# Attention scores of a head pair as two 64-row matmuls, each head with a PSUM bank of its own

## The chip, the cores and the metric

The kernel runs on one core of a Trainium2 chip. The metric is the device time of one execution in microseconds (us). Engines are named as the profile names them: PE (TensorE matmuls), PEld (TensorE weight loads), DVE (VectorE), ACT (ScalarE), POOL (GpSimd), SP (SyncE, which issues the DMAs).

## The reference

Three blocks follow each other. First comes an attention over 2 batches, 8 heads, 768 positions and a head dimension of 64: each query sees the keys within 15 positions of its own, and 24 summary keys (the maximum over blocks of 32 keys) with log(32) added to their scores.

```python
k_sum = k.reshape(B, H, nb, block, D).max(axis=3)
v_sum = v.reshape(B, H, nb, block, D).mean(axis=3)
scores_l = scale * np.matmul(q, k.transpose(0, 1, 3, 2))
scores_s = scale * np.einsum('bhsd,bhnd->bhsn', q, k_sum) + np.log(block)
scores_all = np.concatenate([np.where(mask_l, scores_l, -1e9), scores_s], axis=-1)
a = softmax(scores_all)
out = np.matmul(a, np.concatenate([v, v_sum], axis=2))
```

Then 1536 tokens of width 512 go through an RMS norm, a gated layer (silu(x w_gate) * (x w_val)) w_out with 1536 hidden units, and a second layer (s * relu(x w_in)^2 + b) w_out with 2048 hidden units. All is float32, the weights are float64 in memory.

## The kernel before

**Work units.** A token tile i is 128 queries of one batch (12 tiles). A unit is a token tile and a pair of heads (4 pairs, so 48 units). The queries and keys of a pair lie with the first head in partitions 0 to 63 and the second in 64 to 127. A unit's key window has 192 columns: 24 summary keys, 8 empty ones, two times 16 neighbours and the tile's own 128 keys.

**Scores (`emit_a`, line 317).** The queries lie in `qz` (line 79), two buffers of [128, 2, 4, 128]: for head e of the pair, the other head's 64 rows are zero, set once in `consts` (lines 113 to 115). `load_q` (line 268) fills a tile's queries with two DMAs of 64 rows. Per unit, line 328 issues two float32 matmuls over all 128 rows, one per head, into the two halves of one PSUM bank. A float32 matmul that isn't a transpose stands in the trace as two weight loads and two matmul records, so a unit has four of each. Then `top` (line 333, on DVE) adds the mask, scales and takes the row maximum of each head, and `exps` (line 339, on ACT) does the exponentials and their sums.

**Order of the work.** `attn` (line 405) runs over steps s. A step first issues, three steps late, the transposes of unit s-3 (`emit_b`, line 348, copied out by line 354 on ACT or 352 on DVE), then, six steps late, the products with the values (`emit_c`, lines 367 to 369), and yields; then it issues the scores of unit s and yields again. At each yield the main loop (line 640) calls `run_due`, which issues the work that `after(d, ...)` put d calls later: `top` at the second call after the scores, `exps` at the third. It then may issue a transpose of a normed tile (`emit_e`, line 396) and one group of 12 matmuls of the gated layer (lines 469 to 472). Each engine works through its own instructions in the order of issue.

**PSUM banks.** The scores take banks 0, 1 and 2 in turn, and from the 20th yield on banks 0 and 1 in turn (lines 631 and 644). A unit's matmuls wait until the `top` of the unit that last used their bank has read it. The transposes use 3, 4 and 5 (later 3 and 4), the value products 6 and 7, the layers 2 and 5.

**Other work of the engines.** On DVE: block maxima of the keys (line 276) and sums of the values (line 292), the norm (379, 389), half of the split of normed tokens (402), and the conversion of float64 weights (192 to 194). On ACT: lines 183, 214, 354, 383, 400, 509. On POOL: 216, 313, 358, 359, 385. After the attention's last unit only the two layers run, up to the end.

```python
ps = ps_s()
pv = [ps[:, e * KC:(e + 1) * KC] for e in range(2)]
for e in range(2):
    nc.tensor.matmul(pv[e], qz[i % 2][:, e, pr], kW(i // NTL, pr, t), start=True, stop=True)
```

Of the kernel before, what the change touches and what calls it, by code (L numbers as in the profile page):

```python
# [9 lines left out]
F32 = mybir.dt.float32  # L10
# [3 lines left out]
AF = mybir.ActivationFunctionType  # L14
ALU = mybir.AluOpType
AX = mybir.AxisListType
PSUM = bass.MemoryType.PSUM
# [3 lines left out]
NPAIR = NH // 2  # L21
NTL = SEQ // 128
# [3 lines left out]
KC = 192  # L26
# [10 lines left out]
def kernel(ctx: ExitStack, tc: tile.TileContext, q_t, k_t, v_t, v_w, w_gate, w_val, w_out, w_in2, w_out2, rms_g, s2, b2, out):  # L37
    nc = tc.nc
    scale = 1.0 / math.sqrt(HD)
# [16 lines left out]
    psp = pool("ps", 1, space=PSUM)  # L56

    def banks(*ids):
        """tiles of the PSUM banks ids, in turn"""
        turn = [0]  # L60

        def take():
            i = ids[turn[0] % len(ids)]
            turn[0] += 1
            return psp.tile([128, 512], F32, tag=f"b{i}", name=f"b{i}")
        return take
# [1 line left out]
    def r(ap):  # L68
        return ap.bitcast(F32R)

# [1 line left out]
    ident = const.tile([128, 128], F32, name="ident")  # L72
    mone = const.tile([128, NH], F32, name="mone")
    mhalf = const.tile([128, 1], F32, name="mhalf")
# [1 line left out]
    gbc = const.tile([128, DM], F32, name="gbc")  # L76
    sbc = const.tile([128, 1], F32, name="sbc")
    bbc = const.tile([128, 1], F32, name="bbc")
    qz = [const.tile([128, 2, NPAIR, 128], F32, name=f"qz{i}") for i in range(2)]
    part = const.tile([128, NSUB * 4 * SUB], F32, name="part")  # L80

    def big():
        return hgp.tile([128, NSUB * 2 * SUB], F32, tag="hg", name="hg")

    # keys and values of both batches lie where the products of the MoE come to lie later
    store = [big() for _ in range(5)] + [part[:, i * 3072:(i + 1) * 3072] for i in range(2)]
    kst = [t.rearrange("p (j c) -> p j c", c=KC) for t in (store[0], store[3], store[5])]
    vst = [t.rearrange("p (t a c) -> p t a c", t=3, a=NPAIR) for t in (store[1], store[2], store[4], store[6])]
# [2 lines left out]
    def kW(b, pr, t):  # L91
        j = (b * NPAIR + pr) * NTL + t
        return kst[j // 16][:, j % 16]

    def kpieces(b, pr):
        """runs of tiles of a pair's keys in one store: (store, slot, first tile, tiles)"""
        j = (b * NPAIR + pr) * NTL
        out, t = [], 0
        while t < NTL:
            n = min(NTL - t, 16 - (j + t) % 16)  # L100
            out.append((kst[(j + t) // 16], (j + t) % 16, t, n))
            t += n
        return out
# [6 lines left out]

    def consts():
        make_identity(nc, ident)
        for z in qz:
            nc.vector.memset(z[64:128, 0], 0.0)
            nc.vector.memset(z[0:64, 1], 0.0)
        for st in kst:
            nc.vector.memset(st[:, :, NS:BLK], 0.0)
        m = masks[1]
        nc.gpsimd.memset(m, 0.0)
        nc.gpsimd.memset(m[:, 0:NS], math.log(BLK) / scale)  # L120
        nc.gpsimd.memset(m[:, NS:BLK], NEG / scale)
        band(m, BLK, WIN, -WIN)
        band(m, BLK + WIN, WIN, 128)
        band(m, 64, 128, 0)
        for i, o in ((0, BLK), (2, BLK + WIN)):
            nc.vector.tensor_copy(masks[i], m)
            nc.vector.memset(masks[i][:, o:o + WIN], NEG / scale)
        nc.gpsimd.memset(mhalf, -0.5)
        nc.gpsimd.memset(mone, -1.0)
# [3 lines left out]
        nc.sync.dma_start(out=sbc, in_=s2.rearrange("(o d) -> o d", o=1).broadcast_to([128, 1]))  # L133
        nc.sync.dma_start(out=bbc, in_=b2.rearrange("(o d) -> o d", o=1).broadcast_to([128, 1]))

# [1 line left out]
    later = [[] for _ in range(8)]  # L137

    def after(d, fn):
        later[d].append(fn)  # L140
# [4 lines left out]
        for fn in due:  # L145
            fn()

# [1 line left out]
    order = []  # L149
    for m in range(KF):  # L150
        order.append(("s1", m))
# [26 lines left out]
        raw_t[i] = t  # L178

    def w_scale(i):  # L180
        """high words as float32 with their exponent moved: 2^-112 leaves five bits of it"""
        a = wap.tile([128, 512], F32, tag="wa", name="wa")
        nc.scalar.activation(out=a, in_=raw_t[i][:, :, 1].bitcast(F32), func=AF.Copy, scale=2.0 ** -112)
        a_t[i] = a

    def w_bits(i):
        """float32 of the float64 words: 23 bits of mantissa, the last one rounded to odd"""
        t = raw_t.pop(i)
        lo, hi = t[:, :, 0], t[:, :, 1]
        ai = a_t[i].bitcast(I32)  # L190
        ops = [
            lambda: nc.vector.tensor_scalar(out=ai, in0=ai, scalar1=3, scalar2=1, op0=ALU.logical_shift_left, op1=ALU.bitwise_or),
            lambda: nc.vector.scalar_tensor_tensor(out=ai, in0=hi, scalar=-0x80000000, in1=ai, op0=ALU.bitwise_and, op1=ALU.bitwise_or),  # L193
            lambda: nc.vector.scalar_tensor_tensor(out=ai, in0=lo, scalar=29, in1=ai, op0=ALU.logical_shift_right, op1=ALU.bitwise_or),  # L194
        ]
        pend[i] = ops

        def one():
            if ops:
                ops.pop(0)()  # L200
        one()
        if busy[0]:
            after(1, one)
            after(3, one)
        else:
            one()
            one()
# [27 lines left out]
                prog[j] += 1  # L235

    def w_ahead(part):
        """the weights' own work, between the work of the tokens"""
        i = used[0]
        if part == 0:  # L240
            w_to(i + 8, i + 7, 0, i + 5)
        elif part == 1:
            w_to(i + 8, 0, i + 6, 0)
# [6 lines left out]
        used[0] += 1  # L250
        return ready.pop(i)

# [1 line left out]
    vt_t = {}  # L254

    def load_k(b, pr):
# [9 lines left out]
        nc.sync.dma_start(out=vA[b][t].rearrange("p a c -> p (a c)"), in_=v_w[b, t])  # L266

    def load_q(i):
        z = qz[i % 2]
        for e in range(2):  # L270
            nc.sync.dma_start(out=z[64 * e:64 * e + 64, e].rearrange("p a c -> p (a c)"), in_=q_t[i, 64 * e:64 * e + 64])

    def prep_k(b, pr):
        ks = smallp.tile([128, NS], F32, tag="ks", name="ks")
# [10 lines left out]
        return vt_t[b][:, c0:c0 + 512].rearrange("p (a c) -> p a c", a=NPAIR)  # L285

    def prep_v(b, pr):
        """block means of the values, per column of the transposed values"""
        if pr == 0:
            nc.gpsimd.memset(vsums(b, 0), 0.0)  # L290
        vs = vsums(b, 1)[:, :, 0:NS]
        nc.vector.tensor_reduce(out=vs[:, pr], in_=vt_t[b][:, pr * SEQ:(pr + 1) * SEQ].rearrange("p (c i) -> p c i", i=BLK),
                                axis=AX.X, op=ALU.add)
        if pr == NPAIR - 1:
            for h in range(2):
                p0 = 64 * h
                nc.scalar.activation(out=vsums(b, 0)[p0:p0 + 64, :, p0:p0 + NS], in_=vs[p0:p0 + 64], func=AF.Copy, scale=1.0 / BLK)
# [16 lines left out]

    P_t, PT_t, X_t, xn_t, sm_t = {}, {}, {}, {}, {}

    def emit_a(i, pr, ps_s):
        t = i % NTL
        mk = masks[0 if t == 0 else 2 if t == NTL - 1 else 1]
        if pr == 0:  # L320
            sm_t[i] = smallp.tile([128, 2, NH], F32, tag="sm", name="sm")
        sm = sm_t[i]
        P = (tmpp.tile([128, 512], F32, tag="tmp", name="P") if i else wlp.tile([128, 512], F32, tag="wl", name="P"))
        P = P[:, 0:2 * KC].rearrange("p (e c) -> p e c", e=2)
        ps = ps_s()
        pv = [ps[:, e * KC:(e + 1) * KC] for e in range(2)]
        for e in range(2):
            nc.tensor.matmul(pv[e], qz[i % 2][:, e, pr], kW(i // NTL, pr, t), start=True, stop=True)  # L328

        def top():  # L330
            for e in range(2):
                h = 2 * pr + e
                nc.vector.tensor_tensor_reduce(out=P[:, e], in0=pv[e], in1=mk, op0=ALU.add, op1=ALU.min,
                                               scale=-scale, scalar=3.0e38, accum_out=sm[:, 0, h:h + 1])

        def exps():
            for e in range(2):
                h = 2 * pr + e
                nc.scalar.activation(out=P[:, e], in_=P[:, e], func=AF.Exp, scale=-1.0,  # L339
                                     bias=sm[:, 0, h:h + 1], accum_out=sm[:, 1, h:h + 1])  # L340
        after(1, top)
        after(2, exps)
        P_t[i, pr] = P

    def emit_b(i, pr, ps):
        P = P_t.pop((i, pr)).rearrange("p e c -> p (e c)")
# [55 lines left out]
        after(1, lambda: nc.vector.tensor_tensor(out=r(x[:, 1, :, c0:c0 + 128]), in0=pv, in1=x[:, 0, :, c0:c0 + 128], op=ALU.subtract))  # L402

    def attn(ps_s, ps_t, ps_x):
        """half a unit per step; yields the token tile that it completes"""
        loads = [lambda t=t: load_vw(0, t) for t in range(3, NTL)]
        loads += [lambda pr=pr: load_k(1, pr) for pr in range(NPAIR)]
        loads.append(lambda: load_vt(1))
# [31 lines left out]
        for s in range(n + LC):  # L440
# [14 lines left out]
                        emit_d(i)  # L455
            yield done
            if s < n:
                emit_a(*us[s], ps_s)
                i, pr = us[s]
                if pr == NPAIR - 1 and i + 2 < NT:  # L460
                    load_q(i + 2)
                yield

# [1 line left out]
    def mm12(ps, w, act):  # L465
        hi, lo = w
        for kk in range(4):
# [4 lines left out]
            nc.tensor.matmul(ps, r(hi[:, kk * 128:(kk + 1) * 128]), r(act(kk, 1)), start=False, stop=kk == 3)  # L472

    def slot(part):
        """what follows a group of products: the weights ahead, then older groups' work"""
        run_due()
        if phase:
            part = phase[0] = 1 - phase[0]
        if not busy[0]:
            w_ahead(part)  # L480
# [6 lines left out]
        return big().rearrange("p (s e c) -> p s e c", s=NSUB, e=2)  # L487

    def two(ps, dst, bias=None):
        """ps (+ bias) as a float32r pair"""  # L490
        if bias is None:
            nc.scalar.activation(out=r(dst[0]), in_=ps, func=AF.Copy)
            nc.vector.tensor_tensor(out=r(dst[1]), in0=ps, in1=dst[0], op=ALU.subtract)
# [2 lines left out]
            nc.vector.scalar_tensor_tensor(out=r(dst[1]), in0=ps, scalar=bias, in1=dst[0], op0=ALU.add, op1=ALU.subtract)  # L496

    def moe(x, ps_m):
        """x: a tile of (hi, lo) per part of the tokens"""
        hs, gs, y = {}, {}, []  # L500
        yp = part.rearrange("p (m s c) -> p m s c", m=KD, s=NSUB)
        op = part.rearrange("p (t c) -> p t c", t=NT)
# [112 lines left out]
        for kind, m in order:  # L615
            yield from {"s1": s1, "s2": s2, "s3": s3, "s4": s4}[kind](m)

# [1 line left out]
    consts()  # L619
    x = [xyp.tile([128, 2, KD, SUB], F32, tag="xy", name="x")]  # L620
    load_k(0, 0)
# [6 lines left out]
    for t in range(3):  # L628
        load_vw(0, t)
    load_small()  # L630
    m_banks, s_banks, t_banks = [banks(2, 5)], [banks(0, 1, 2)], [banks(3, 4, 5)]

    def ps_t():
        return t_banks[0]()
# [49 lines left out]
def _layout(q, k, v, moe_w_gate, moe_w_val, moe_w_out, moe_rms_g, moe2_w_in, moe2_w_out, moe2_s, moe2_b):  # L684
# [2 lines left out]
    c = np.ascontiguousarray  # L687

    def heads(a):
        # [b, h, s, d] -> [b, (e d), pair, s]  # L690
        return a.reshape(NB, NPAIR, 2, SEQ, HD).transpose(0, 2, 4, 1, 3).reshape(NB, 128, NPAIR, SEQ)

    qt = heads(q).reshape(NB, 128, NPAIR, NTL, 128).transpose(0, 3, 1, 2, 4)
# [63 lines left out]
```

## Time and profile before

| what | value |
|---|---|
| time, median of 2 runs (lowest to highest) | 663.58 us (663.47 to 663.69) |
| profiled execution: span from first to last instruction | 662.4 us |
| what the times have around that span (663.58 - 662.4) | 1.2 us |
| PE busy in the span | 645.8 us (97%) |
| DVE, ACT, POOL busy | 402.2, 272.6, 137.3 us |
| mean granted TensorE clock | 0.997 |
| score matmuls (line 328), first and last start | 7.8 and 113.9 us |

The profiled execution has a span and no time of its own beside it; the 1.2 us is what the measured runs have more than this span. Busy times of one engine can overlap with another's. A matmul's record is longer than its pitch, because matmuls are pipelined: the pitch is read from the starts.

### The profile page before, as it was taken

How to read it: one execution, taken by the hardware profiler on the slowest of the kernel's cores; microseconds unless marked ns; L12 is line 12 of the kernel's file. 1: busy time of each engine (PE TensorE's matmuls, PEld its weight loads, DVE VectorE, ACT ScalarE, POOL GpSimd, SP SyncE). 2: the span in 40 equal slices, each digit the busy share in tenths (PEclk: the TensorE clock that was granted, in tenths of full speed). 3: DMA queues.
4: the chain of work that ended last, by engine and by line, in shares of the span. 5: the costliest groups of instructions: out<-in, count | busy, mean ns of one | idle time of the engine just before them, and what ended most of it. 6: DMA issues, size and time to landing. Idle time of an engine off the chain costs nothing.

```text
span 662.4 us, 8488 instructions
## 1 busy us (share of the span) xinstructions
PE 645.8 (97%) x3140; PEld 547.7 (83%) x3140; DVE 402.2 (61%) x763; ACT 272.6 (41%) x610; POOL 137.3 (21%) x157
## 2 busy tenths in 40 slices
PE   3989999999999999999999999999999999999998
PEld 3988999888888888888888888888888888888886
DVE  7699777469751355554455767882178637854632
ACT  3888767235433333321233335552455035403400
POOL 2365633213211111111111111110221022102100
PEclk9999999999999999999999999999999999999999
DMA  9995230014332121222222212113022202220022
GB/s 299 301 347 167 65 120 9 0 45 147 95 96 63 33 64 64 64 63 66 63 69 62 71 53 64 65 63 96 0 96 64 95 13 84 65 63 1 1 95 96
DMA packets 23243, 56.13 MB, mean 85 GB/s; under 512 B 2465, under 2 KB 8865, under 8 KB 23201
## 3 DMA queue, kind: packets, MB, share of 16 engines
q1 hardware_dynamic: 23200, 55.58, 26.4%
q8 instruction: 25, 0.41, 0.3%
q14 instruction: 18, 0.14, 0.1%
HBM read 52.43 MB, written 3.15 MB: 84 GB/s over the span
## 4 chain that ended last, share of the span: by engine, by line
PE 91%; ACT 2%; DMA 2%; DVE 2%; POOL 1%; issue 1%; SPq 0%; POOLq 0%
PE b L469 21%; PE b L470 21%; PE b L472 21%; PE b L601 7%; PE b L604 7%; PE b L602 7%; PE b L328 3%; DMA qz<-in_q_t_dram 2%; PE b L348 1%; ACT P L339 1%; PE b L367 1%; PE b L369 1%; PE b L368 1%; PE b L396 1%; ACT PT L354 0%
## 5 line engine op out<-in xcount | busy, mean ns | idle before, releaser
L216 POOL TENSOR_TENSOR wl<-wa,wh 128x512 fp32r<-128x512 f32 x68 | 90.5, 1338 | 418.4 <-ACT wh L214 328.8
L469 PE MATMUL b<-x,wh 128*128 128x512 f32 x288 | 113.1, 393 | 0.0
L470 PE MATMUL b<-x,wl 128*128 128x512 f32 x288 | 112.1, 389 | 0.0
L214 ACT ACTIVATE wh<-wa 128x512 fp32r<-128x512 f32 x68 | 41.5, 626 | 90.8 <-PE b L604 45.5
L472 PE MATMUL b<-x,wh 128*128 128x512 f32 x288 | 77.1, 389 | 0.0
L602 PE MATMUL b<-wl,hg 128*128 128x512 f32 (+1 forms) x196 | 75.1, 385 | 0.0
L601 PE MATMUL b<-wh,hg 128*128 128x512 f32 (+1 forms) x196 | 75.1, 385 | 0.0
L469 PE MATMUL b<-y,wh 128*128 128x512 f32 x192 | 74.7, 389 | 0.0
L470 PE MATMUL b<-y,wl 128*128 128x512 f32 x192 | 74.7, 389 | 0.0
L583 DVE SCALAR_TENSOR_TENSOR b<-u,sbc 128x512 f32<-128x512 f32 x48 | 50.7, 1056 | 35.6 <-ACT u L582 35.6
L472 PEld LDWEIGHTS b<-x,wh 128*128 128x128 f32 x288 | 54.1, 188 | 11.3
L470 PEld LDWEIGHTS b<-x,wl 128*128 128x128 f32 x288 | 54.1, 188 | 11.0
L469 PEld LDWEIGHTS b<-x,wh 128*128 128x128 f32 x288 | 54.1, 188 | 11.0
L469 PE MATMUL b<-hg,wh 128*128 128x512 f32 x144 | 56.0, 389 | 0.0
L470 PE MATMUL b<-hg,wl 128*128 128x512 f32 x144 | 56.0, 389 | 0.0
L496 DVE SCALAR_TENSOR_TENSOR hg<-b,bbc,hg 128x512 fp32r<-128x512 f32 x48 | 35.9, 749 | 28.2 <-ACT hg L495 28.2
L604 PE MATMUL b<-wh,hg 128*128 128x512 f32 (+1 forms) x196 | 51.5, 385 | 0.0
L472 PE MATMUL b<-y,wh 128*128 128x512 f32 x192 | 51.3, 389 | 0.0
L610 DVE TENSOR_TENSOR part<-b,part 128x512 f32<-128x512 f32 (+1 forms) x37 | 24.4, 673 | 43.4 <-PE b L604 43.4
L495 ACT ACTIVATE hg<-b,bbc 128x512 fp32r<-128x512 f32 x48 | 33.0, 688 | 43.0 <-DVE b L583 43.0
L194 DVE SCALAR_TENSOR_TENSOR wa<-raw,wa 128x512 int32<-128x512 int32 x68 | 49.2, 724 | 2.1
L193 DVE SCALAR_TENSOR_TENSOR wa<-raw,wa 128x512 int32<-128x512 int32 x68 | 49.1, 722 | 2.3
(93 smaller groups left out, 1075.0 us busy)
## 6 DMA issues: line engine op xcount, KB each, us to landing
raw<-in_w_out_dram SPq DMA_DIRECT2D x28, 512.0 KB, 3.5
raw<-in_w_in_dram SPq DMA_DIRECT2D x16, 512.0 KB, 3.5
raw<-in_w_gate_dram SPq DMA_DIRECT2D x12, 512.0 KB, 3.8
raw<-in_w_val_dram SPq DMA_DIRECT2D x12, 512.0 KB, 3.5
hg<-in_v_w_dram SPq DMA_DIRECT2D x9, 512.0 KB, 7.7
qz<-in_q_t_dram SPq DMA_DIRECT2D x24, 128.0 KB, 4.8
vt<-in_v_t_dram SPq DMA_DIRECT2D x8, 384.0 KB, 6.5
out_dram<-part SPq DMA_DIRECT2D x11, 256.0 KB, 2.0
```

The source lines that it names most:

```text
L193: lambda: nc.vector.scalar_tensor_tensor(out=ai, in0=hi, scalar=-0x80000000, in1=ai, op0=ALU.bitwise_and, op1=ALU.bitwise_or),
L194: lambda: nc.vector.scalar_tensor_tensor(out=ai, in0=lo, scalar=29, in1=ai, op0=ALU.logical_shift_right, op1=ALU.bitwise_or),
L214: nc.scalar.activation(out=r(h), in_=a, func=AF.Copy)
L216: nc.gpsimd.tensor_tensor(out=r(lo), in0=a, in1=h, op=ALU.subtract)
L469: nc.tensor.matmul(ps, r(hi[:, kk * 128:(kk + 1) * 128]), xh, start=kk == 0, stop=False)
L470: nc.tensor.matmul(ps, r(lo[:, kk * 128:(kk + 1) * 128]), xh, start=False, stop=False)
L472: nc.tensor.matmul(ps, r(hi[:, kk * 128:(kk + 1) * 128]), r(act(kk, 1)), start=False, stop=kk == 3)
L496: nc.vector.scalar_tensor_tensor(out=r(dst[1]), in0=ps, scalar=bias, in1=dst[0], op0=ALU.add, op1=ALU.subtract)
L583: after(0, lambda u=u, ps=ps: nc.vector.scalar_tensor_tensor(out=ps, in0=u, scalar=sbc[:, 0:1], in1=u, op0=ALU.mult, op1=ALU.mult))
L601: nc.tensor.matmul(acc, gh, r(ws[e][0][:, cs]), start=e == 0, stop=False)
L602: nc.tensor.matmul(acc, gh, r(ws[e][1][:, cs]), start=False, stop=False)
L604: nc.tensor.matmul(acc, r(ge[e][:, 1]), r(ws[e][0][:, cs]), start=False, stop=e == 3)
```

## The change

Both heads' queries lie in one buffer without zeros, loaded by one DMA per tile. At every even unit, `emit_a` takes both score banks and issues the scores of two units (pairs pr0 and pr0+1): for each pair, head 0 from partitions 0 to 63 into bank `pe[0]`, and head 1 from partitions 64 to 127 into bank `pe[1]`. The second unit's maxima are issued one `run_due` after the first's, its exponentials likewise, so that they come one call earlier than before, where its scores were issued one step later. The scores rotate over banks 0 and 1 from the start. Docstrings and comments also go; they are left out here.

```diff
-    qz = [const.tile([128, 2, NPAIR, 128], F32, name=f"qz{i}") for i in range(2)]
+    qz = [const.tile([128, NPAIR, 128], F32, name=f"qz{i}") for i in range(2)]
...
-        for z in qz:
-            nc.vector.memset(z[64:128, 0], 0.0)
-            nc.vector.memset(z[0:64, 1], 0.0)
...
     def load_q(i):
-        z = qz[i % 2]
-        for e in range(2):
-            nc.sync.dma_start(out=z[64 * e:64 * e + 64, e].rearrange("p a c -> p (a c)"), in_=q_t[i, 64 * e:64 * e + 64])
+        nc.sync.dma_start(out=qz[i % 2].rearrange("p a c -> p (a c)"), in_=q_t[i])
...
-    def emit_a(i, pr, ps_s):
+    def emit_a(i, pr0, ps_s):
...
-        ps = ps_s()
-        pv = [ps[:, e * KC:(e + 1) * KC] for e in range(2)]
-        for e in range(2):
-            nc.tensor.matmul(pv[e], qz[i % 2][:, e, pr], kW(i // NTL, pr, t), start=True, stop=True)
+        pe = [ps_s() for _ in range(2)]
+        for j in range(2):
             for e in range(2):
+                rows = slice(64 * e, 64 * e + 64)
+                nc.tensor.matmul(pe[e][:, j * KC:(j + 1) * KC], qz[i % 2][rows, pr0 + j], kW(i // NTL, pr0 + j, t)[rows],
+                                 start=True, stop=True)
...
+        def soft(j):
+            pr = pr0 + j
...
+            def top():
+                for e in range(2):
+                    h = 2 * pr + e
+                    nc.vector.tensor_tensor_reduce(out=P[:, e], in0=pe[e][:, j * KC:(j + 1) * KC], in1=mk, op0=ALU.add,
+                                                   op1=ALU.min, scale=-scale, scalar=3.0e38, accum_out=sm[:, 0, h:h + 1])
...
-        after(1, top)
-        after(2, exps)
+            after(1 + j, top)
+            after(2 + j, exps)
...
             if s < n:
-                emit_a(*us[s], ps_s)
                 i, pr = us[s]
+                if pr % 2 == 0:
+                    emit_a(i, pr, ps_s)
...
-    m_banks, s_banks, t_banks = [banks(2, 5)], [banks(0, 1, 2)], [banks(3, 4, 5)]
+    m_banks, s_banks, t_banks = [banks(2, 5)], [banks(0, 1)], [banks(3, 4, 5)]
```

## Rows read from the trace of the kernel before

**Rows 1.** The page: span, engines' busy time, granted clock in 40 slices.
```profile
span 662.4 us, 8488 instructions
...
PE 645.8 (97%) x3140; PEld 547.7 (83%) x3140; DVE 402.2 (61%) x763; ACT 272.6 (41%) x610; POOL 137.3 (21%) x157
...
PEclk9999999999999999999999999999999999999999
```

**Rows 2.** Busy time by stretch: us, PE, PEld, DVE, ACT, POOL, clock, DMA, GB/s.
```profile
25.00:45.00 20.00, 20.00 (x161) 19.71 (x160) 15.46 (x56) 19.06 (x67) 11.82 (x18) 1.00 0.94 303
45.00:58.00 13.00, 9.79 (x76) 9.28 (x75) 12.60 (x40) 9.90 (x34) 6.18 (x10) 1.00 1.00 356
58.00:115.00 57.00, 56.97 (x396) 52.93 (x395) 44.48 (x147) 41.26 (x138) 28.18 (x40) 1.00 0.19 58
115.00:640.00 525.00, 525.00 (x2343) 435.55 (x2343) 306.68 (x454) 191.02 (x334) 85.53 (x68) 1.00 0.20 62
```

**Rows 3.** Waits of 0 to 125 us, those of the score matmuls.
```profile
PE b L328 <- DMA qz<-in_q_t_dram: 10.1, 2, 7.8
...
PE b L328 <- DVE sm L333: 3.2, 3, 2.1
```

**Rows 4.** Timeline of PE around 81 and, cut after 2 and 3 records, 82.5 us.
```profile
80.84 0.82 PE L328 MATMUL b<-part,qz 128*128 128x192 f32 x4
81.50 0.49 PE L348 MATMUL b<-ident,P 128*128 128x128 f32 x3
...
82.44 0.54 PE L328 MATMUL b<-part,qz 128*128 128x192 f32 x2
...
82.44 0.71 PE L328 MATMUL b<-part,qz 128*128 128x192 f32 x3
```

**Rows 5.** Timeline of the weight loads around 82 us.
```profile
81.94 0.30 PEld L368 LDWEIGHTS b<-hg,PT 128*128 128x128 f32 x2
82.16 0.30 PEld L369 LDWEIGHTS b<-hg,PT 128*128 128x128 f32 x2
```

**Rows 6.** Line 328, one form: duration ns min/median/max.
```profile
L328 PE MATMUL b<-part,qz x64: 326/326/382, 60.2 to 113.9; 128*128 128x192 f32 x64
```

**Rows 7.** Line 328 alone by stretch: us, PE busy (records), PEld, clock, DMA, GB/s.
```profile
15.78:58.00 42.22, 19.67 (x85) 14.41 (x86) 0.96 0.97 325
58.00:115.00 57.00, 19.56 (x92) 14.22 (x91) 1.00 0.19 58
```

**Rows 8.** Timeline, DVE's maxima and the next scores at 23 and 55 us.
```profile
23.33 0.08 DVE L333 DVE_READ_ACCUMULATOR2_ANT sm<- 128x1 f32 x1
...
23.58 0.38 PE L328 MATMUL b<-hg,qz 128*128 128x192 f32 x1
...
55.07 0.34 DVE L333 CUSTOM_DVE_ANT_0 P<-b,mask 128x192 f32<-128x192 f32 x1
...
55.62 0.08 DVE L333 DVE_READ_ACCUMULATOR2_ANT sm<- 128x1 f32 x1
...
55.75 0.43 PE L328 MATMUL b<-hg,qz 128*128 128x192 f32 x1 [0.70 <-DVE sm L333]
```

**Rows 9.** Timeline around 75 us: DVE's work ahead of a maximum, and scores.
```profile
74.90 0.55 DVE L192 TENSOR_SCALAR wa<-wa 128x512 int32<-128x512 int32 x1
...
75.49 0.77 DVE L193 SCALAR_TENSOR_TENSOR wa<-raw,wa 128x512 int32<-128x512 int32 x1
...
76.02 0.87 PE L328 MATMUL b<-hg,qz 128*128 128x192 f32 x4
```

**Rows 10.** Timeline of the start: memsets, DVE's wait, the two waits for queries.
```profile
0.89 0.48 DVE L114 MEMSET qz<- 64x512 f32 x1 [0.89 <-PEq L744]
...
7.27 0.95 DVE L276 TENSOR_REDUCE ks<-hg 128x24 f32<-128x768 f32 x1 [1.53 <-DMA hg<-in_k_t_dram]
...
7.83 4.18 PE L328 MATMUL b<-hg,qz 128*128 128x192 f32 x12 [7.83 <-DMA qz<-in_q_t_dram]
...
15.78 1.61 PE L328 MATMUL b<-hg,qz 128*128 128x192 f32 x4 [2.22 <-DMA qz<-in_q_t_dram]
```

More of the change, by code (lines that the diff above doesn't have):

```diff
@@ L315 @@
     P_t, PT_t, X_t, xn_t, sm_t = {}, {}, {}, {}, {}
-    def emit_a(i, pr, ps_s):
+    def emit_a(i, pr0, ps_s):
         t = i % NTL
         mk = masks[0 if t == 0 else 2 if t == NTL - 1 else 1]
-        if pr == 0:
+        if pr0 == 0:
             sm_t[i] = smallp.tile([128, 2, NH], F32, tag="sm", name="sm")
         sm = sm_t[i]
-        P = (tmpp.tile([128, 512], F32, tag="tmp", name="P") if i else wlp.tile([128, 512], F32, tag="wl", name="P"))
-        P = P[:, 0:2 * KC].rearrange("p (e c) -> p e c", e=2)
-        ps = ps_s()
-        pv = [ps[:, e * KC:(e + 1) * KC] for e in range(2)]
-        for e in range(2):
-            nc.tensor.matmul(pv[e], qz[i % 2][:, e, pr], kW(i // NTL, pr, t), start=True, stop=True)
-        def top():
-            for e in range(2):
[L332 to L340, printed above, removed]
-        after(1, top)
-        after(2, exps)
-        P_t[i, pr] = P
@@ new lines, in emit_a, with exps @@
+        pe = [ps_s() for _ in range(2)]
+        for j in range(2):
+            for e in range(2):
+                rows = slice(64 * e, 64 * e + 64)
[3 more added lines that the diff above has]
+            pr = pr0 + j
+            P = (tmpp.tile([128, 512], F32, tag="tmp", name="P") if i else wlp.tile([128, 512], F32, tag="wl", name="P"))
+            P = P[:, 0:2 * KC].rearrange("p (e c) -> p e c", e=2)
+            def top():
[3 more added lines that the diff above has]
+                                                   op1=ALU.min, scale=-scale, scalar=3.0e38, accum_out=sm[:, 0, h:h + 1])
+            def exps():
+                for e in range(2):
+                    h = 2 * pr + e
+                    nc.scalar.activation(out=P[:, e], in_=P[:, e], func=AF.Exp, scale=-1.0,
+                                         bias=sm[:, 0, h:h + 1], accum_out=sm[:, 1, h:h + 1])
+            after(1 + j, top)
+            after(2 + j, exps)
+            P_t[i, pr] = P
@@ L345, in emit_b @@
+        soft(0)
+        soft(1)
     def emit_b(i, pr, ps):
```

## The prediction

> **What bounds the kernel now.** I read the page first. PE is busy 645.8 of 662.4 us and the granted clock stands at its upper level, 2.4 GHz, in every slice [rows 1]. A busy share of 97% doesn't say that every saved PE nanosecond counts, so the second view is busy time by stretch. It shows three regimes. From 115 us to the end only the layers run, and PE is busy all the time; the change touches nothing there. From 58 to 115 us attention and layer are mixed: PE is busy 56.97 of 57.00 us, DVE 44.48 (78%) and ACT 41.26 (72%); here PE is the limit and the others have room. From 45 to 58 us it is DVE, busy 12.60 of 13.00 us, while PE has 3.2 us of idle time; and from 25 to 45 us PE (20.00 of 20.00) and ACT (19.06) are both full [rows 2]. The third view, the waits, says what PE's idle time is: the scores wait 10.1 us for queries, at the start, and 3.2 us for DVE, which has not yet read the bank that they are to overwrite [rows 3]. So PE issues in order and, from 15.78 us on, is held up only by that second wait. What the change gives PE after 58 us shortens the kernel one for one; what it gives before that is mostly taken by ACT or DVE; and each new PE wait, wherever it is after 15.78 us, lengthens it one for one.
>
> **The change, part by part.**
>
> *Score matmuls on PE.* The number of instructions stays: 96 calls, 192 weight loads and 192 matmul records, each still 192 columns. What can change is how closely they follow. Now a record takes 0.326 us [rows 6] but the next starts 0.163 us later: the third of a unit ends at 0.71, the second at 0.54, so 0.17 by the rounded rows [rows 4], and a whole unit goes from 80.84 to 81.50, 0.66 us, to the next instruction, or 0.165 per record. A group of two units, eight records, so costs 8 x 0.163 = 1.30 us. In two row halves the matmul of head 1 can run beside one of head 0. The issue order is head 0 twice, head 1 twice, head 0 twice, head 1 twice, and in order only the second record of a head can overlap the first of the other, so eight records need five pitches, 5 x 0.163 = 0.81 us. The weight loads don't get fewer: back to back they follow each other every 0.11 us (two pairs start 0.22 us apart [rows 5]), and 8 x 0.11 = 0.88 us is more than 0.81. With overlap a group then takes some 0.88 us and saves 0.42 us; bounds are 0 (the halves don't overlap) and 0.65 (four pitches, if loads run beside each other too and order didn't matter). I take 0.42, because the load pitch is the nearest row that limits it.
>
> *Going into the row halves and out again.* Each group stands between full-array work, so there are 24 times two switches. No row shows a switch of array shape. What the rows show is that a change of operation alone (scores to transposes) costs nothing, 0.66 us for four pitches of 0.163 [rows 4]: the lower bound is 0. The upper bound is that nothing overlaps across it: the tail of a record beyond its pitch, 0.326 - 0.163 = 0.163 us, plus a weight load that is no longer hidden, 0.19 us (the second of two loads 0.11 apart ends at 0.30), so 0.35 us. I take 0.11, one load pitch, nearer to the row that shows nothing. Two of them cost 0.22 per group, and the group's saving is 0.42 - 0.22 = 0.20 us. The Trainium skill ("TensorEngine Tiling (Array Packing)", Key Properties) speaks against this step: changing the tiling mode drains the engine. No run here shows it yet; with a drain priced by the tail of a record and a load, that rule is the second rival below.
>
> How many groups count: after 58 us there are 92 records (88 would be 11 groups, with the remainder of a unit already begun), in the stretch before it 85 [rows 7]. So 11 groups in the PE-bound stretch: 11 x 0.20 = **-2.2 us**. The groups between 15.78 and 58 us I count as 0: ACT has 0.94 us of room in 20 and DVE 0.40 in 13 [rows 2], so at most about 1 us could come through.
>
> *Two banks for two units at once.* This adds a wait. Now unit u+2 waits for the maxima of unit u, issued two run_due calls earlier, and unit u+3 for those of u+1. In the new order the next group waits for the maxima of both units, and those of the second are issued one call later than the first's. What is queued behind that wait is all of PE's later work: the transposes, value products and layer matmuls. A unit's maxima take from 55.07 to 55.70, 0.63 us, on DVE. At 23.58, 30.91, 37.95, 47.19, 50.93 and 55.75 us PE came to the group's first matmul 0.17, 0.05, 0.40, 0.06, 0.43 and 0.05 us after the first unit's maxima were done (the first and the last of the six are shown [rows 8]). There the second unit's 0.63 us no longer fits: 6 x 0.63 - 1.16 = 2.6 us of new waits at the least if they added up. They don't quite, since a PE that has waited comes later to the next group. If one other DVE operation of 0.7 us stands between the two maxima at five of these places, it is 2.6 + 3.5 = 6 us. I take **+2.0 us**, near the lower end because DVE's order mostly puts the two maxima closer than now; bounds 0 and 6. After 58 us there is more room. The tight case looks like 76 us: the weight conversions of 0.55 and 0.77 us stand between the maxima (74.98 to 76.18), and scores want the bank at 76.02 [rows 9]. If they stay ahead of the second maxima, PE waits 76.18 + 0.55 - 76.02 = 0.7 us; if not, nothing. Four of eleven groups look like this (scores at 60.21, 66.26, 76.02 and 92.20), so 0 to 2.8 us; I take **+0.7 us**.
>
> *The rest.* Four memsets of 0.48 us leave DVE before 3.3 us; DVE afterwards sits idle 1.53 us for keys at 7.27 [rows 10], so this is hidden, and nothing is lost if that cover goes. The query load becomes one DMA with the same bytes. The second tile's scores, PE's last start-up wait, come at 15.78 when its queries land [rows 10], and the DMA engines are full up to then, so bytes and not issues set it: 0, at best -0.6 us for one issue less on SP's queue. That the first group now needs two pairs of keys, and all of tile 0 comes earlier or later by a unit, lies ahead of this same wait. The exponentials of every second unit come one call earlier, which helps ACT's order but not its load: 0.
>
> **Sum.** -2.2 + 2.0 + 0.7 = +0.5 us on the span of 662.4, and 1.2 us around it: 664.1 us, against a median of 663.58. That is no change; this kernel's measurement tells about 2%, 13 us, from no change.
>
> **The rivals.**
> *Switches for nothing.* The halves overlap and the switches cost little: 11 x 0.42 = 4.6 us off after 58 us, about 1 us before, and 2.0 to 2.7 of waits kept: 662.4 - 5.6 + 2.4 + 1.2 = 660.4 us. For it: changes of operation are free in the rows, and loads run ahead under matmuls [rows 4, 5]. Against it: PE gets faster but DVE is at 78% even in the good stretch, so more of the gain turns into waits. The Trainium skill ("TensorE: Matmul & The Clock Gate", Part 3) has matmuls in different row groups start some 4 ns apart; no row here shows it, and by it the five pitches hold and the load pitch limits.
>
> *The array drains at each switch (slower).* Place: the edges of each group; price: 0.22 us (tail 0.163 plus the 0.06 by which a load must precede its matmul, an estimate from half the load pitch) to 0.35 us per switch. It decides from 0.21 us on, where two switches eat the 0.42 saved. All 22 groups after 15.78 us pay, since PE is dense there: with overlap 22 x (0.44 to 0.70 - 0.42) = 0.4 to 6.2 us and the bank waits of 2.7: 667 to 672 us. Without overlap 22 x 0.70 = 15.4, with 0 to 2: 679 us and more. I put it at 670 us. For it: nothing in the rows excludes a drain, a record's tail is as long as its pitch. Against it: the wait for DVE of 3.2 us would hide part.
>
> *The halves don't run together.* Then the change does not do what it says; eight records stay at 1.30 us and only the bank waits come: 662.4 + 1.2 + 2.7 = 666.3 us, up to 670 if these waits come at the upper end. For it: the loads of a float32 call stand between its two records, so the order gives little to overlap. Against it: the operands lie in separate rows and separate banks.
>
> **How the numbers follow.** Forecast (within 662 to 666): 0.45. Switches for nothing: 0.25. Drain: 0.20. No overlap, or larger bank waits: 0.10. Low end 659, a little below the first rival with 0.42 saved; high end 672, the drain with overlap at its full price. Outside lie the drain without overlap (0.07), overlap better than the load pitch (0.05) and bank waits over 6 us. For faster by 2% the time would have to be under 650.3, where 24 x 0.65 = 15.6 us would have to come through in full: 0.01. Slower by 2% is 676.9, the drain without overlap: 0.04. Within 2%: 0.95. As the likeliest case by itself has both signs, its own range is 661 to 667.
>
> **What would show it.** In the profile after: the score records read 64 rows, still 192 of them; a group's first to last record start spans about 0.8 us with the second head's records beginning while the first head's run (overlap) or 1.14 us at 0.163 each (none). The gap from the full-array matmul before a group to the group's first record, and from its last to the next, tells the switch: 0.16 or less for free, 0.3 and more for a drain. The wait of the scores for the maxima, 3.2 us now, should grow to 5 or 6, before 58 us above all. The last score should start near 114 us and the layers after it should keep their pitch at the same clock. I am wrong if that wait stays or grows past 10 us, if PE no longer fills the stretch up to the last score, or if records of one half are themselves longer than 0.326 us.

## The result, and the profile after

The changed kernel takes 669.38 us (668.89 to 669.88) against 663.58: a ratio of 1.0086, 95% interval 1.0057 to 1.0115. That is 5.8 us slower, inside the 2% that counts as no change and inside the forecast range, but above the 661 to 667 us that I gave the likeliest case. Its profiled execution spans 667.1 us, 4.7 more than before.

In the new file the scores are line 323, the maxima 334, the exponentials 340, the transposes 351, the value products 370 to 372, the norm's Square 386 (ACT), its two POOL steps 387 and 388, and the scaling by their result 392 (DVE). First the scores alone, by stretch, with the columns of [rows 7]:

```profile
15.78:58.00 42.22, 10.72 (x80) 7.56 (x76) 0.92 0.86 319
58.00:118.00 60.00, 12.40 (x96) 8.87 (x96) 1.00 0.17 54
```

PE is busy with scores for 23.1 us, where [rows 7] had 39.2, so the row halves do their work. The timeline of PE shows how; the last two lines are the same group cut after 0.02 and 0.28 us:

```profile
86.37 0.39 PE L372 MATMUL b<-hg,PT 128*128 128x64 f32 x2
86.68 0.92 PE L323 MATMUL b<-part,qz 64*128 64x192 f32 x8
87.53 0.55 PE L351 MATMUL b<-ident,P 128*128 128x128 f32 x3
...
86.68 0.43 PE L323 MATMUL b<-part,qz 64*128 64x192 f32 x2
...
86.68 0.60 PE L323 MATMUL b<-part,qz 64*128 64x192 f32 x4
```

Two records start within 0.02 us, one of each head, and the next two follow together: eight records go in four pairs, and the next instruction starts 0.85 us after the first. So the time was probably lost elsewhere. The waits from 0 to 125 us say where (us in total, times, longest):

```profile
DVE xn L392 <- POOL ss L388: 15.8, 11, 2.5
...
PE b L323 <- DVE sm L334: 8.8, 8, 2.2
PE b L323 <- DMA qz<-in_q_t_dram: 8.3, 2, 8.0
```

The scores' wait for DVE went from 3.2 us [rows 3] to 8.8, and DVE's own largest wait is for POOL at the norm's scaling; the same wait of the kernel before is 6.4 us:

```profile
DVE xn L389 <- POOL ss L385: 6.4, 9, 2.0
```

Busy time by stretch, with the columns of [rows 2]:

```profile
25.00:45.00 20.00, 17.47 (x137) 16.01 (x138) 14.24 (x51) 17.13 (x60) 10.67 (x15) 0.91 0.93 330
45.00:58.00 13.00, 10.84 (x82) 9.84 (x78) 10.49 (x30) 9.34 (x30) 7.01 (x12) 0.87 0.68 268
62.00:118.00 56.00, 53.70 (x391) 46.70 (x391) 44.32 (x134) 38.85 (x131) 27.30 (x39) 1.00 0.18 57
```

Between 25 and 45 us PE, DVE and ACT all do less than before, not one more: nobody is the limit, they wait for each other. Even after 58 us, where PE was the limit, it now has gaps (first the kernel before, then the changed one):

```profile
58.00:125.00 67.00, 66.97 (x461) 61.96 (x460) 49.10 (x154) 44.81 (x148) 31.58 (x46) 1.00 0.16 49
...
58.00:125.00 67.00, 62.19 (x457) 54.31 (x457) 52.86 (x163) 45.18 (x154) 30.80 (x44) 1.00 0.15 49
```

PE idles 4.8 of these 67 us, where it idled 0.03. From 15.78 to 58 us it idles 6.0 us instead of 3.4 (busy 36.27 and 38.86 of 42.22). The granted clock is 0.91 and 0.87 in the two stretches before 58 us, where it was 1.00 [rows 2]: two stretches there run at the lower level, 1.2 GHz. One of them, after PE had waited 1.43 us for DVE at 39.44:

```profile
41.10:44.30 3.20, 3.20 (x19) 3.20 (x17) 2.96 (x12) 2.61 (x10) 2.70 (x3) 0.50 1.02 419
```

The second is at 51.30 to 54.60, after a wait of 2.16 us at 49.8. At most half of each, 1.6 us, is lost by that. The kernel before has one such stretch too, from 15.78 to 19.20 us, behind its wait for queries, so the change adds one. A wait by itself does not bring it about: the kernel before waited 2.07 us for DVE at 47.19, and its clock stayed at 1.00 [rows 2].

What happens in nine of the twelve token tiles is best seen in the timeline of ACT, POOL, DVE and PE from 34.8 to 39.4 us of the changed kernel:

```profile
34.82 0.45 ACT L340 ACTIVATE P<-P,sm 128x192 f32<-128x192 f32 x1
...
35.26 0.45 ACT L340 ACTIVATE P<-P,sm 128x192 f32<-128x192 f32 x1
...
35.70 0.59 ACT L386 ACTIVATE b<-xn 128x512 f32<-128x512 f32 x1
...
36.50 0.19 POOL L387 TENSOR_SCALAR ss<-ss 128x1 f32<-128x1 f32 x1 [1.75 <-ACT b L386]
36.78 0.55 POOL L388 TENSOR_TENSOR ss<-ss,mhalf 128x1 f32<-128x1 f32 x1
...
37.36 0.85 DVE L392 SCALAR_TENSOR_TENSOR xn<-xn,ss,gbc 128x512 f32<-128x512 f32 x1 [1.71 <-POOL ss L388]
38.14 0.34 DVE L334 CUSTOM_DVE_ANT_0 P<-b,mask 128x192 f32<-128x192 f32 x1
...
39.44 0.43 PE L323 MATMUL b<-hg,qz 64*128 64x192 f32 x1 [1.43 <-DVE sm L334]
```

The second unit's two exponentials, issued a call earlier than before, stand ahead of the Square on ACT; POOL starts late; DVE idles 1.71 us ahead of the scaling; the maxima, queued behind it, start at 38.14; and PE, whose next group overwrites both banks, starts it at 39.44. In the kernel before, at the same tile, the Square ran before any exponential of that call and DVE had a unit's maxima to do meanwhile:

```profile
34.47 0.59 ACT L383 ACTIVATE b<-xn 128x512 f32<-128x512 f32 x1
...
35.22 0.35 DVE L333 CUSTOM_DVE_ANT_0 P<-b,mask 128x192 f32<-128x192 f32 x1
...
36.14 0.85 DVE L389 SCALAR_TENSOR_TENSOR xn<-xn,ss,gbc 128x512 f32<-128x512 f32 x1 [0.29 <-POOL ss L385]
```

So there were three theories: **order** (this chain), **banks** (two banks freed only after the second unit's maxima) and **switch** (the row halves cost PE more than they save).

### The profile page after: what moved, and what is told of

Read it like the earlier page. It is cut to its first block, busy times and chain, and to the rows that moved or that the text cites. A ratio compares the mean times of both kernels' runs of the same rounds, so it can differ in the third digit from the quotient of the medians.

```text
span 667.1 us, 8448 instructions
## 1 busy us (share of the span) xinstructions
PE 643.4 (96%) x3140; PEld 537.2 (81%) x3140; DVE 402.3 (60%) x759; ACT 271.8 (41%) x610; POOL 137.4 (21%) x157
## 4 chain that ended last, share of the span: by engine, by line
PE 85%; ACT 5%; DVE 5%; issue 1%; DMA 1%; SPq 1%; POOL 1%; ACTq 0%; POOLq 0%
PE b L473 21%; PE b L474 21%; PE b L476 21%; PE b L605 7%; PE b L606 7%; PE b L608 7%; ACT P L340 3%; DVE P L334 2%; PE b L323 1%; DMA qz<-in_q_t_dram 1%; DVE xn L392 1%; ACT b L386 1%; POOL ss L388 1%; PE b L351 1%; ACT x L403 0%
## 5 line engine op out<-in xcount | busy, mean ns | idle before, releaser
L340 ACT ACTIVATE P<-P,sm 128x192 f32<-128x192 f32 x96 | 42.5, 445 | 22.3 <-DVE sm L334 21.0
L191 DVE SCALAR_TENSOR_TENSOR wa<-raw,wa 128x512 int32<-128x512 int32 x68 | 49.3, 725 | 2.1
```

## The experiments

All ratios are to the kernel before, timed beside each run. An edit is one to the changed kernel unless said otherwise.

### Undoing the row halves alone

The zero-padded queries, with their four memsets and two loads per tile, come back as in the kernel before; of that edit only the matmuls are shown.

```diff
...
-                rows = slice(64 * e, 64 * e + 64)
-                nc.tensor.matmul(pe[e][:, j * KC:(j + 1) * KC], qz[i % 2][rows, pr0 + j], kW(i // NTL, pr0 + j, t)[rows],
+                nc.tensor.matmul(pe[e][:, j * KC:(j + 1) * KC], qz[i % 2][:, e, pr0 + j], kW(i // NTL, pr0 + j, t),
```

Expected: 

> The changed kernel, but its score matmuls over all 128 rows with zero-padded queries as before (two query DMAs and four memsets again); same grouping, same two banks, same order. Theory 'banks' (the group of two units frees both banks late) and theory 'order' (the second unit's exponentials now stand ahead of the norm's Square on ACT, so POOL's result is late and DVE idles at the norm's scaling, ahead of the maxima): the cost is in grouping and order, so this stays at 669 or rises to 674 us as eight records take 1.30 us again. Theory 'switch' (the row halves themselves cost, by draining the array): 663 to 666 us.

Measured: 671.87 us, ratio 1.0125 (1.0103 to 1.0147). It did not get faster, as "switch" asked (663 to 666 us), so "switch" falls. DVE's wait for POOL is still 14.2 us, so "order" and "banks" both stand. The timeline of PE, one group:

```profile
110.11 0.39 PE L376 MATMUL b<-part,PT 128*128 128x64 f32 x2
110.34 1.52 PE L327 MATMUL b<-part,qz 128*128 128x192 f32 x8
111.69 0.49 PE L355 MATMUL b<-ident,P 128*128 128x128 f32 x3
```

From the start of the two records ahead to the instruction behind the group it takes 111.69 - 110.11 = 1.58 us; with row halves 87.53 - 86.37 = 1.16. A group saves 0.42 us net, switches included, and 24 of them would save 10 us of PE time. But only a group that finds both banks free goes in pairs. Where PE had to wait for the maxima, DVE reads the second head's bank 0.28 us after the first's, and the two heads start as far apart (DVE, then PE, in the changed kernel):

```profile
79.89 0.34 DVE L334 CUSTOM_DVE_ANT_0 P<-b,mask 128x192 f32<-128x192 f32 x1
...
80.17 0.35 DVE L334 CUSTOM_DVE_ANT_0 P<-b,mask 128x192 f32<-128x192 f32 x1
...
80.30 0.70 PE L323 MATMUL b<-hg,qz 64*128 64x192 f32 x3 [0.96 <-DVE sm L334]
...
81.42 0.50 PE L473 MATMUL b<-x,wh 128*128 128x512 f32 x1
```

This group takes 1.12 us to the next instruction instead of 0.85, so 0.15 us of the saving is left. Of the 21 groups from 17 us on, 10 start like this. Yet the time differs by only 0.0039 of 663.6, 2.6 us, with intervals that overlap: such groups and the waits swallow the rest.

### Taking the exponentials back, or moving the scaling

```diff
-            after(2 + j, exps)
+            after(2 + 2 * j, exps)
```

Expected: 

> The changed kernel with the second unit's exponentials issued one call later, where they stood before the change (after(4) instead of after(3)); nothing else. Theory 'order': DVE's wait for POOL at the norm's scaling falls from 15.8 towards 6.4 us, the scores' wait for DVE from 8.8 to about 5, time 664 to 666 us. Theory 'banks': the bank wait stays near 8.8 us and the time at 668.5 to 670.5 us.

Measured: 661.99 us, ratio 0.9977 (0.9964 to 0.9989), and better than "order" had asked for, although the waits fell less than it had asked: DVE's wait for POOL is 10.1 us, the scores' wait for DVE 6.9.

```diff
-        after(3, lambda: nc.vector.scalar_tensor_tensor(out=xn, ...
+        after(4, lambda: nc.vector.scalar_tensor_tensor(out=xn, ...
```

Expected: 

> The changed kernel with the norm's scaling on DVE issued one call later (after(4) instead of after(3)); nothing else. Theory 'order': POOL has a call more, DVE's wait there falls below 6 us, and the time to 663 to 666 us. Theory 'banks': the bank wait stays near 8.8 us, time 668 to 670.5 us.

Measured: 663.99 us, ratio 1.0006 (0.9994 to 1.0019), DVE's wait for POOL 8.7 us, the scores' wait 7.0. The wait for POOL did not fall as far as expected, but the time did. Both edits take 5 us or more away without touching the banks.

### The two exponentials and the Square change places

The tightest test changes ACT's order in that one call of nine tiles; the instruction orders of PE, DVE and POOL stay as they were.

```diff
-        after(2, rms)
+        later[2].insert(0, rms)
```

Expected: 

> The changed kernel in which one pair of ACT instructions changes places: in the call in which both fall, the norm's Square is issued ahead of the second unit's two exponentials instead of behind them. All else, the banks too, is as in the changed kernel. Theory 'order': this is the whole cause, so DVE's wait for POOL falls from 15.8 to 10 us or less and the time to 661 to 664.5 us, as when the exponentials went back a call (661.99). Rival 'ACT and DVE order as a whole' (the exponentials come too early for several others, not the Square alone): 665 to 668 us. Theory 'banks': 668 to 670 us.

Measured: 662.02 us, ratio 0.9977 (0.9964 to 0.9990). The same tile in its timeline:

```profile
34.29 0.60 ACT L386 ACTIVATE b<-xn 128x512 f32<-128x512 f32 x1
...
34.90 0.45 ACT L340 ACTIVATE P<-P,sm 128x192 f32<-128x192 f32 x1
...
35.95 0.85 DVE L392 SCALAR_TENSOR_TENSOR xn<-xn,ss,gbc 128x512 f32<-128x512 f32 x1 [0.83 <-POOL ss L388]
...
38.03 0.43 PE L323 MATMUL b<-hg,qz 64*128 64x192 f32 x1 [0.56 <-DVE sm L334]
```

The Square now runs first, DVE idles 0.83 us instead of 1.71, and PE's wait at this group falls from 1.43 to 0.56 us. The waits of the whole run: DVE for POOL 9.8 us, scores for DVE 6.7. An exchange of places on ACT, which costs no instruction, is worth 1.0086 - 0.9977 = 0.0109, 7.2 us, by the two intervals some 2 us more or less. That is more than the change lost: the interval of this run lies below 1. The tile shows the chain, but most of PE's time comes back later:

```profile
58.00:125.00 67.00, 65.89 (x474) 57.43 (x473) 52.09 (x156) 44.12 (x149) 31.59 (x46) 1.00 0.15 49
```

After 58 us PE idles 1.1 us instead of 4.8. From 15.78 to 58 us it idles 5.8 instead of 6.0, as the wait at 47.5 is now 2.77 us, and has one stretch at the lower clock there instead of two.

### The fourth corner: full rows with the exponentials back

The first edit (full rows) and the second (exponentials back) together: of the four combinations of row halves or full rows with early or late exponentials, the one still missing.

Expected: 

> Full-array, zero-padded score matmuls with the changed kernel's grouping and banks, and the second unit's exponentials one call later: the fourth corner beside the changed kernel (669.38), full rows (671.87) and exponentials back (661.99). If the row halves are worth their PE time (0.3 us for each of 24 groups) once the order no longer hides it, this is 4 to 7 us above 661.99, so 666 to 669 us. If most of PE's gain is still lost in waits, 663 to 665 us; that would also say that the grouping by itself is harmless next to before (663.57).

Measured: 665.80 us, ratio 1.0024 (1.0013 to 1.0034), below what full PE worth would have given and above the harmless case. With it the change comes apart, in ratios times 663.6: grouping, banks and the second unit's earlier maxima together +1.6 us (1.0024), row halves -3.1 us (0.9977 - 1.0024), the early exponentials +7.2 us. That these add up to +5.7 us is no test, as each step starts where the one before ends; by the intervals they are known to some 0.7, 1 and 2 us. With full rows, the early exponentials cost 1.0125 - 1.0024, 6.7 us, so no dependence of their price on the row halves is seen.

### The banks

```diff
-            after(1 + j, top)
+            after(1, top)
```

Expected: 

> The changed kernel with the maxima of both units issued in the same call (after(1) for both), so that both banks are free one call earlier; exponentials as in the changed kernel. Theory 'banks': the scores' wait for DVE falls from 8.8 to below 4 us and the time to 663 to 666 us. Theory 'order': DVE still idles some 15 us for POOL, the time stays at 668 us or more.

Measured: 667.78 us, ratio 1.0063 (1.0043 to 1.0084), the scores' wait still 8.8 us, DVE's for POOL 14.5. The time lies a little below where "order" wanted it and far above where "banks" did; its interval overlaps that of the changed kernel, so as to the maxima themselves it is inconclusive. Next, the three edits together (maxima in one call, exponentials back, scaling later), and the same without the first.

Expected: 

> The changed kernel with the three edits together: both units' maxima in the same call, the second unit's exponentials one call later, the norm's scaling one call later. Theory 'order' and 'banks' both: what is left of the scores' wait (6.9 us with the exponentials alone) falls below 4 us and the time to 657 to 661 us. If the three edits act on the same wait, it stays at 661 to 663 us.

Measured: 659.71 us, ratio 0.9935 (0.9920 to 0.9950); the scores' wait is 3.9 us, DVE's for POOL 3.3.

Expected: 

> The changed kernel with the second unit's exponentials one call later and the norm's scaling one call later, but the maxima in their two calls. If the early maxima bring something beside the order, this lies above the 659.71 of all three, at 660.5 to 662 us; if they bring nothing, 659.5 to 660 us.

Measured: 659.90 us, ratio 0.9945 (0.9924 to 0.9967), waits of 4.6 and 4.5 us. The early maxima bring nothing that can be measured. "Banks" in the form "free them one call earlier" falls. That holding two banks costs something is not excluded: grouping with its banks cost 1.6 us.

### The order in the kernel before

One edit to the kernel before, which puts two exponentials ahead of the Square there:

```diff
-        after(2, exps)
+        after(2 + (pr + 1) % 2, exps)
```

Expected: 

> The kernel before, with one edit: the exponentials of every pair with an even number run one call later, which puts two of them ahead of the norm's Square on ACT in the call in which it falls, as in the changed kernel; scores, banks, grouping and row halves as before. Theory 'order': DVE's wait for POOL at the norm's scaling rises from 6.4 to 12 us or more, and the time to 667 to 671 us with none of the change's other parts. If the order hurts only together with the group that holds both banks, DVE's wait rises but the time stays at 663 to 665.5 us.

Measured: 665.30 us, ratio 1.0019 (1.0008 to 1.0029). DVE's wait for POOL rose from 6.4 to 9.7 us only, the scores' wait was 2.1 us. So the order alone costs about 1.3 us in the old arrangement, a fifth of its price in the new one, which is what the second case expected. Even that is not shown to come by way of DVE: in the profiled execution PE idles no longer than before (12.1 us of the first 125, against 13.5), but has a second stretch at the lower clock, from 47.80 to 51.20 us. It is no exact copy either, since here the exponentials come late rather than early. The timelines above fit the small price: the old DVE has a unit's maxima to do while POOL works, the new one has none, and the next group's maxima stand behind the scaling.

### Issuing the scores head by head

```diff
-        for j in range(2):
-            for e in range(2):
+        for e in range(2):
+            for j in range(2):
```

Expected: 

> The changed kernel with the four score matmuls of a group issued head by head (head 0 of both pairs, then head 1 of both) instead of pair by pair. If PE keeps strict order, head 1 can start only beside the last record of head 0: a group's first to last record start spans about 1.0 to 1.1 us instead of 0.6, and the busy time of the scores grows. If each row half takes its instructions independently, the spans stay at 0.6 us. Time 669 to 675 us.

Measured: 669.26 us in a single run, beside 663.88, so no different from the changed kernel as far as one run tells. The timeline of PE, one group cut after 0.015 and after 0.90 us:

```profile
92.78 0.44 PE L323 MATMUL b<-hg,qz 64*128 64x192 f32 x2
...
92.78 0.60 PE L323 MATMUL b<-hg,qz 64*128 64x192 f32 x4
93.21 0.50 PE L323 MATMUL b<-part,qz 64*128 64x192 f32 x4
93.64 0.33 PE L351 MATMUL b<-ident,P 128*128 128x128 f32 x1
```

Head 1's first record stands behind four of head 0 in the program, two of them with keys in `part`; in the trace the first four records all read keys in `hg`, and two of these start within 0.015 us, one of each head. The group again takes 0.86 us. Each row half takes its own instructions.

### Spreading DVE's work

The three edits with the scaling at after(5), and the second batch's value sums, their transposes and copies a step later; the last part of the edit is:

```diff
...
-            at(22 + pr, prep_v, 1, pr)
-        at(26, means, 1)
+            at(23 + pr, prep_v, 1, pr)
+        at(27, means, 1)
...
-            at(27 + t, prep_v3, 1, t)
+            at(28 + t, prep_v3, 1, t)
```

Expected: 

> The three edits together, with the norm's scaling two calls later instead of one, and the second batch's value sums, their transposes and copies one step later, so that DVE's densest stretch is spread. If what is left of the scores' wait (3.9 us) comes from DVE's load between 40 and 58 us, 657.5 to 659.3 us; if it comes from the banks alone, 659.4 to 660.5 us.

Measured: 656.42 us, ratio 0.9886 (0.9865 to 0.9907), better than expected, and 1.1% below the kernel before, which is inside the 2% that count as no change but with an interval that leaves 1 out. The scores' wait for DVE is 2.6 us, DVE's for POOL no longer among its largest. By stretch:

```profile
45.00:58.00 13.00, 11.87 (x93) 10.13 (x91) 12.78 (x39) 10.38 (x36) 6.31 (x11) 1.00 0.67 264
58.00:115.00 57.00, 56.98 (x423) 50.17 (x423) 45.62 (x141) 40.58 (x139) 28.78 (x42) 1.00 0.16 53
```

PE is full again after 58 us, as in [rows 2], but handles 423 records there instead of 396, and the clock stays up. Which of the two added moves brought the 3.3 us over the three edits was not tried apart. Last, the same with full rows:

Expected: 

> The spread version (656.42) with full-array, zero-padded score matmuls instead of row halves: what the row halves are worth once DVE, ACT and POOL no longer hold PE up. A group takes 1.47 us on PE with full rows and 1.06 with row halves, 0.41 us, and 11 to 22 of the 24 groups lie where PE is dense: if that comes through, 661 to 665.5 us. If PE's gain is still mostly swallowed, as with the exponentials alone put back (3.8 us came through), 659 to 661 us.

Measured: 662.14 us, ratio 0.9972 (0.9960 to 0.9985). The row halves are worth 0.9972 - 0.9886, 5.7 us, here: more than twice the 2.6 us that came through in the order of the change, and 0.42 us for some 14 of the 24 groups. By their intervals, the 5.7 is known to some 1.6 us and the 2.6 to some 2.4. It fits that in the spread version only 3 of the 21 groups from 17 us on start their heads 0.27 us apart, and 3 more by 0.13 to 0.20, where the changed kernel had 10.

## Why the prediction was right or wrong

**The direction and the size.** The forecast of no change within 2% held and the range held, but by luck: its high end was set by a drain at the switches, and 669.4 us came about in another way. That the drain rival's 670 us is so near is chance too. The sum was +0.5 us and the measured change +5.8. It was not one of my rivals: the halves do run together, the switches are cheap, and without the early exponentials the kernel would have been 0.23% faster than before. Term by term I had -2.2 for the row halves, +2.7 for the two banks and 0 for the exponentials; measured are -3.1, +1.6 and +7.2. So the miss lies in the last term.

**Score matmuls on PE: right in kind, undersized.** I took a saving of 0.42 us per group from overlap and 0.22 us for two switches, 0.20 net; measured is 0.42 net for a group that finds its banks free, and 0.15 for one that does not. What failed here is the order of issue: I let only the second record of a head overlap the first of the other, and priced the eight weight loads at 0.11 us each, 0.88 in all. The loads of a group take 0.63 us:

```profile
86.68 0.63 PEld L323 LDWEIGHTS b<-part,qz 64*128 64x128 f32 x8
```

and the records go in pairs, 0.007 us apart, so the five pitches and the load pitch do not hold, and my upper bound of four pitches, 0.65 us before the switches, is what is seen.

**The switches: right.** The second of two value-product records starts 0.11 us after the first: 86.48 before a group of row halves, 110.22 before one of full rows. The group follows after 0.20 us in the one case and 0.12 in the other. On the way out, the raw starts give 0.254 us from the last record to the next instruction against 0.163. That is about 0.09 us for each edge; another 0.05 lies inside the group, where the second pair starts 0.267 us after the first, and the second record of full rows 0.218. In all it is 0.65 - 0.42 = 0.23 us per group, where I had taken 0.22, and far from twice the 0.21 at which the drain would have decided. The Trainium skill ("TensorEngine Tiling (Array Packing)", Key Properties) has a change of the tiling mode drain the engine; the trace agrees that an edge costs something, with 0.09 us beside it. Whether that is a drain, no run here shows.

**What counts and what is swallowed: right in part.** I counted the groups before 58 us as 0, since ACT and DVE are full there, and wrote that DVE's share would turn gain into waits. Of at most 10 us of PE time, 2.6 came through in the order of the change. But I held that PE stays the limit after 58 us, and it idles 4.8 us there, 3.7 of them ahead of the last score. That PE no longer fills the stretch up to the last score was one of my signs of being wrong, and it came true.

**Two banks for two units at once: about right.** I expected the scores' wait to go from 3.2 to 5 or 6 us; it went to 8.8, and to 6.7 with the exchange on ACT, so 2.1 of the 5.6 us more belong to the order. The price, +2.7 us, is near the measured +1.6. Freeing both banks a call earlier left the wait at 8.8 and brought 1.6 us, which is within the intervals.

**The exponentials: wrong, and this is the step that failed.** I wrote that the exponentials of every second unit come one call earlier, "which helps ACT's order but not its load: 0". Measured +7.2 us, and only together with the grouping: in the kernel before, a like order cost 1.3. I moved two ACT instructions and asked who waits for them, not what they now stand in front of. The chain was to be seen before: ACT 95% busy from 25 to 45 us [rows 2], the Square in that call, POOL behind it, DVE's scaling behind POOL, and the maxima behind the scaling.

**Elsewhere.** The start brought little that lasts, as forecast: the scores' wait for queries fell from 10.1 [rows 3] to 8.3 us, but PE is busy 7.2 of the first 17 us, where it was 6.9. The clock I read as at its upper level in every slice, but a 9 there is 90% or more, and [rows 7] has 0.96 before 58 us: the kernel before has a stretch at the lower level at 15.78. I expected the clock to stay; the changed kernel has two such stretches, the spread version none. Of my chances, 0.04 for slower by 2% does not go with 0.07 for a drain without overlap, which lies beyond it at 679 us.

## What to carry to other kernels

When work moves to another place in an engine's queue, list what it now stands ahead of, and follow that victim across engines to the end: two exponentials of 0.45 us ahead of a Square in nine tiles cost 7.2 us here, as DVE idled behind POOL in front of the maxima that PE needed. A faster instruction stream on the fullest engine shows up in the time only where the others keep up, so a change like this is judged together with the order around it: the same row halves were worth 2.6, 3.1 and 5.7 us under three orders, of which the first two can't be told apart.

## What the runs showed of the hardware that was not expected

Two 64-row matmuls of float32 in the two row halves run fully beside each other, weight loads included: eight records of 192 columns take 0.85 us from the first to the next instruction, against 1.35 over the full array. The halves do not keep the program's order between them: with all of head 0 issued first, head 1's first record still starts within 0.015 us of head 0's. Where the second head's bank comes free 0.28 us later, its records start that much later, and the group takes 1.12 us. The one edge in and one out of this shape cost about 0.09 us each.
